# Attention over 32 memory slots and a SwiGLU layer: where the normalised x of the second pair of batches is formed

## The chip, the cores and the metric

The kernel runs on one core of a Trainium2 chip. The metric is the device time of one execution in microseconds. The engines are named as in the profile: PE multiplies matrices (PEld loads its weights), DVE is the vector engine, ACT the scalar engine, POOL is GpSimd, and SP issues nearly all DMAs. [...]

## The reference

```python
a   = softmax(phi)                       # 8 batches, 8 heads, 576 tokens, 32 slots
k_m = einsum('bhsm,bhsd->bhmd', a, k)    # memory keys and values, 64 wide
v_m = einsum('bhsm,bhsd->bhmd', a, v)
attn = softmax(q @ k_m.T / 8)            # 576 x 32 for each head
x    = (attn @ v_m), heads side by side  # 4608 tokens x 512
xn   = x / sqrt(mean(x * x) + 1e-6) * rms_g
out  = (silu(xn @ w_gate) * (xn @ w_val)) @ w_out     # 1536 hidden units
```

The kernel never forms x in full. The mean of x squared is a quadratic form of the attention weights `a` with the gram matrix of v_m; the products of v_m with the weights of the layer are formed first and the attention weights, scaled with the inverse root, are applied to those. "Pair 1's x" below means this: transposing the attention weights of a pair (`tp`, `at`), multiplying them by the gram (`xp`), squaring and summing (`ssq`), the inverse root (`rinv`), spreading it over the tokens (`rp`), scaling `at`, and splitting it into a high and a low part (`ath`, `atl`).

## The kernel before

The eight batches form four pairs, 0 to 3. The kernel has two parts.

The first stage goes through the batches. For each one it takes the softmax of phi, forms the kv product (`kvp`, L573 and L588, with `sums` of the exponentials `es`), scales and transposes it (`post1`, L596 to L605; `turn`, L617; `post2`, L627 to L633), and forms the gram (`post3`, L651 to L659). Pairs 2 and 3 leave their memory values and gram in DRAM (`vgd`, `gd`). For pairs 0 and 1 the stage also takes the scores and the softmax over slots (`q_steps`, `score_steps`; the last step, L746, writes the attention weights), and then forms their x with `x_steps`. The attention weights of both pairs stand in two SBUF tiles, a0 and a1. Meanwhile the first two slices of the weights, which come as 64-bit numbers, are read and converted (`convert`, L345 to L403) to a high and a low part.

The sweep has 48 steps. Step i works on one slice of 128 hidden units and one pair: the first 24 steps on pairs 0 and 1, two steps on pair 0, then two on pair 1, and so on; the other 24 on pairs 2 and 3. A step multiplies v_m by the weights (`vp`, L840), splits the result (`xh` on ACT, L853; `xl` on DVE, L854), forms gate and value (`pg`, `pv`, L876), the activation and product (L884, L885) and their split (`hh`, `hl`, L898 and L899). After each two steps the output products (`po`, L918) are added up (`acc`, L925). In the first half of the sweep the other weights are converted too, and attention for pairs 2 and 3 is done in small pieces (`attend_steps`); their attention weights go to DRAM (`a_dram`, L1013). The x of these two pairs comes from DRAM in three fetches (`x2`, L1029) in the course of the sweep, with PSUM from tag `o`, which the output products use as well.

The order is written down as times: each small step is put into a list with a number (`K_AT`, `X_AT`, `XB` and so on, in arbitrary units), the list is sorted, and the framework orders each engine's instructions from it, letting one that is ready pass one that is not. Tiles of one tag share buffers. SBUF and PSUM of the first stage are handed to the sweep tile by tile, when the last user is done; within a pool, memory is laid out in the order in which tags first appear. In `x2` the fetched attention weights take the buffers of `qr`, `qT` and `ex`. The 33 first events of `x_steps` (gram, fetches, transposes, products, squares, inverse root) are put at `XB + XS * number`, the last nine (spreading, scaling, splitting) at `XM + XN`.

Of the kernel before, what the change touches and what calls it, by code (L numbers as in the profile page):

```python
# [8 lines left out]
F32 = mybir.dt.float32  # L9
# [4 lines left out]
ALU = mybir.AluOpType  # L14
# [4 lines left out]
XTTR = True  # L19
WB = 3  # L20
PRM = dict(
    K_AT=[12.08, 15.05, 41.68, 67.52, 100.72, 122.69, 147.6, 167.28],
    KP=0.82,
    POST=[-0.15, 3.05, 3.9, 7.72, 15.27, 21.96],
    P1=4.13,
# [10 lines left out]
    OL=3.83,  # L36
    QO=[-0.32, 1.73, -1.7, 0.7, 1.27, 3.23],
    SO=[3.76, 13.53, 20.6, 28.62],
    X_AT=[102.5, 152.9],
    XP=1.78,  # L40
    LAG=0.79,
    CV=114.79,
# [2 lines left out]
    CP2=0.05,  # L45
    QE=[0, 0],
    CE=[2, 1],
    XE=[28, 29, 14, 13],
    ESN=[3, 3, 2, 3, 3, 3, 2, 3],
    SUM=[1, 0, 1, 0, 2, 1, 2, 1],  # L50
    CA=1,
# [10 lines left out]
    PSW=[1.728, 2.047, 2.009, 2.653, 2.96, 3.24],  # L62
    SU=[1.874, 3.014, 5.716, 6.6, 9.746, 12.208, 13.357, 15.533],
    AO=[0.162, 0.169, 0.192, 0.276, 0.385, 0.474, 0.562, 0.581, 0.59, 0.601, 0.728, 0.804, 1.158, 1.217],
    XB=[17.199, 22.916],
    XS=[0.1086, 0.0359],
    XM=[21.887, 24.858],
    XN=[0.012, 0.176, 0.184, 0.33, 0.33, 0.566, 0.596, 0.699, 0.766],
    LV=[22.571, 24.198],
    CB=1,  # L70
# [20 lines left out]
def kernel(  # L91
# [36 lines left out]
    G = 2  # L128
# [8 lines left out]
    gram = {}  # L137
    gb = persist.tile([P, 2, 2, P], F32, name="gb")
    dram = ctx.enter_context(tc.tile_pool(name="dram", bufs=1, space=bass.MemoryType.DRAM))
    gram_dram = {i: dram.tile([P, 2, 2, 64], F32, name=f"gd{i}") for i in range(G, NP)}  # L140
    a_dram = {i: dram.tile([P, NT, 256], F32, name=f"ad{i}") for i in range(G, NP)}
    rinv = [persist.tile([P, NT], F32, name=f"rinv{i}") for i in range(NP)]
    at_hi, at_lo = {}, {}

# [9 lines left out]
    def split_v(b, vg):  # L154
        pr, j = divmod(b, 2)
        for e in range(2):
            o = e ^ j
            src = vg.rearrange("p (c e) m -> p c e m", e=2)[:, :, o, :]
            hi, lo = vm[pr][:, 0, :, e, o, :], vm[pr][:, 1, :, e, o, :]
            nc.scalar.copy(hi, src)  # L160
            nc.gpsimd.tensor_tensor(out=lo, in0=src, in1=hi.bitcast(F32), op=ALU.subtract)

    def x_steps(pr, a, psum_t, psum_x, fetch=None):
# [4 lines left out]
        def first():  # L168
            st["at"] = persist.tile([P, NT, 2, P], F32, tag="at", name=f"at{pr}")
            ssqs[pr] = persist.tile([P, NT], F32, tag=f"ssq{i}", name=f"ssq{pr}")  # L170
            for par in range(2):
                rows = slice(64 * par, 64 * par + 64)
                (nc.scalar.copy if pr < G else nc.sync.dma_start)(gb[rows, :, :, rows], gram[pr][rows])

        def turn(t0):
            n = min(2, NT - t0)
# [251 lines left out]
    with ExitStack() as c1:  # L428
# [10 lines left out]
            for c in range(2):  # L439
                nc.vector.memset(hmask[32 * g:32 * g + 32, c:c + 1], float(g % 2 == c))  # L440

        a_tiles = [sb.tile([P, NT, 256], F32, name=f"a{i}", bufs=1) for i in range(G)]

        e_bd = [sk.tile([P, HP, NT, 64], F32, name=f"e_bd{i}", bufs=1) for i in range(2)]
        nc.vector.memset(e_bd[0], 0.0)
# [116 lines left out]
        def kv_steps(b):  # L562
# [84 lines left out]
            def post3():  # L647
                pr = b // 2
                if pr not in gram:
                    gram[pr] = sb.tile([P, 2, 2, 64], F32, tag="gram", name=f"gram{pr}", bufs=3)  # L650
                nc.scalar.copy(gram[pr][:, j], st.pop(("vt", b))[1][:, 0, :2])  # L651
                if pr < G:
                    if pr not in vm:
                        new_vm(pr)
                    split_v(b, st.pop(("vg", b)))
                else:
                    nc.sync.dma_start(vg_dram[b], st.pop(("vg", b)))
                    if j:
                        nc.sync.dma_start(gram_dram[pr], gram[pr])  # L659
                        gram[pr] = gram_dram[pr]  # L660
# [37 lines left out]
        def score_steps(pr, s):  # L698
            R = 2 * NT

            def mm():
                qT = st.pop(("qT", pr, s))
                sp = ps.tile([P, 1024], F32, tag="S", name=f"S{pr}_{s}", bufs=PRM["B"][2])
                for t in range(NT):
                    for j in range(2):
                        nc.tensor.matmul(
                            sp[64 * j:64 * j + 64, 64 * t:64 * t + 64],
                            qT[:, t, j::2],
                            st["km", 2 * pr + j][:, s, :],
                            start=True, stop=True,  # L710
                        )
# [12 lines left out]
            def exp():  # L724
                ex = st["ex", pr, s]
                nc.scalar.activation(ex, ex, AF.Exp, scale=SCALE)

            def norm():
                ex = st.pop(("ex", pr, s))
                sm = sb.tile([P, R, 1], F32, tag="sm", name=f"sm{pr}_{s}")  # L730
                how = PRM["SUM"][pr * HP + s]
                if how == 0:
                    nc.vector.tensor_reduce(out=sm, in_=ex, axis=AX.X, op=ALU.add)
                else:
                    half = sb.tile([P, R, M // 2], F32, tag="half", name=f"half{pr}_{s}", bufs=1)
# [10 lines left out]
                nc.gpsimd.tensor_tensor(  # L746
                    out=a_tiles[pr][:, :, 64 * s:64 * s + 64].rearrange("p t (h m) -> p t h m", m=M),
                    in0=ex.rearrange("p (t h) m -> p t h m", h=2),
                    in1=sm.rearrange("p (t h) o -> p t h o", h=2).broadcast_to([P, NT, 2, M]),
                    op=ALU.mult,  # L750
                )
# [39 lines left out]
        for pr in range(G):  # L791
            for s in range(HP):
                t = PRM["S_AT"][pr * HP + s]
                steps = q_steps(pr, s)
                ev.append((t - PRM["QL"] - PRM["OL"] - PRM["QD"][pr * HP + s], lambda pr=pr, s=s: load_q(pr, s)))
                ev.append((t - PRM["QL"] - PRM["OL"], steps[0]))
                ev += place(t - PRM["QL"], PRM["QO"], steps[1:])
                ev += place(t, PRM["SO"], score_steps(pr, s))
            if pr < G:
                ev += [(PRM["X_AT"][pr] + PRM["XP"] * p, f) for p, f in x_steps(  # L800
                    pr, lambda t, pr=pr: a_tiles[pr][:, t], tile_of("tr"), tile_of("kx"))]
        close = K_AT[B - 1] + 6 * PRM["KP"] + 0.1
        ev.append((close, lambda: (c1k.close(), late_weights())))
        w = first_weights()
# [216 lines left out]
    def x2(pr):  # L1021
        got = {}

        def fetch(t):
            def f():
                for tag, t0, n in (("qr", 0, 4), ("qT", 4, 4), ("ex", 8, 1)):
                    if t0 == t:
                        a = sb.tile([P, n, 256], F32, tag=tag, name=f"ain{pr}_{t0}")
                        nc.sync.dma_start(a, a_dram[pr][:, t0:t0 + n])  # L1029
                        for k in range(n):  # L1030
                            got[t0 + k] = a[:, k]
            return f
        steps = x_steps(pr, got.pop, o_tile, o_tile, fetch)
        return [f for _, f in steps]
# [30 lines left out]
            ev.append((p + 2.01 * PRM["PI"], ld))  # L1065
    for a, p in enumerate(PRM["SU"]):
        ev += place(p, PRM["AO"], attend_steps(G + a // HP, a % HP))
    for a in range(NP - G):
        steps = x2(G + a)
        n = len(steps) - 9  # L1070
        ev += [(PRM["XB"][a] + PRM["XS"][a] * x, f) for x, f in enumerate(steps[:n])]
        ev += place(PRM["XM"][a], PRM["XN"], steps[n:])
        ev.append((PRM["LV"][a], lambda a=a: late_vm(G + a)))
    for _, f in sorted(ev, key=lambda e: e[0]):
        f()
# [30 lines left out]
```

## Time and profile before

| | us |
|---|---|
| median of 3 runs (908.34 to 909.11) | 908.46 |
| the profiled execution | 907.8 |
| its span in the trace | 906.0 |
| PE busy | 837.0 |
| DVE busy | 575.7 |
| first kv, attention and x work (first stage) | to about 146 |
| first gate product of the sweep | 154.3 |

A row of a time line gives start, duration, engine, line and operation, tiles as out<-in, and in brackets the engine's idle time before it and what ended that. A row of a group gives line, engine, operation, tiles and shapes, the count, busy us and mean ns of one, then the idle time before. A row of stages gives the window, its length, the busy us (and number of instructions) of PE, PEld, DVE, ACT and POOL, the granted clock of PE, the mean DMA share and GB/s.

### The profile page before, as it was taken

The page shows a single profiled execution, that of the slowest core. Times are in us where ns is not written, and L with a number is a line of the kernel's source. Part 1 is how long each engine was busy: PE and PEld are TensorE (multiplying, and loading weights), DVE is VectorE, ACT ScalarE, POOL GpSimd, SP SyncE. Part 2 cuts the span into 40 slices and gives each one's busy share as a digit, 9 for nine tenths or more (in the row PEclk, how much of TensorE's full clock was granted, in tenths as well). Part 3 has the DMA queues.
Part 4 walks back from the last instruction along what each step waited for, and adds up shares of the span by engine and source line. Part 5 has one row for each costly group of instructions (what it writes and reads, how often), then busy time and mean ns, then how long its engine had stood idle before and what let it go on. Part 6 is the DMA issues. An engine that isn't in the chain of part 4 may idle for free.

```text
span 906.0 us, 15847 instructions
## 1 busy us (share of the span) xinstructions
PE 837.0 (92%) x6207; PEld 744.5 (82%) x6207; DVE 575.7 (64%) x994; ACT 420.2 (46%) x717; POOL 326.2 (36%) x274
## 2 busy tenths in 40 slices
PE   4998485899998899999999999999999999999997
PEld 4776474788986798888898997799899999999996
DVE  5577959896788777877855656532445455454543
ACT  2666334787765355664642443254424333233330
POOL 3464735553636245344532331411212121121120
PEclk9899787999999999999999999999999999999999
DMA  8986554454445332543413133501204013040046
GB/s 277 337 278 209 201 166 120 168 146 107 164 133 162 101 119 84 152 114 103 140 57 129 52 88 118 121 31 47 94 1 140 1 47 93 1 140 1 1 114 142
DMA packets 81506, 106.41 MB, mean 117 GB/s; under 512 B 34324, under 2 KB 52248, under 8 KB 81432
## 3 DMA queue, kind: packets, MB, share of 16 engines
q1 hardware_dynamic: 81432, 105.41, 37.6%
q8 instruction: 49, 0.80, 0.4%
q14 instruction: 25, 0.20, 0.1%
HBM read 73.93 MB, written 31.46 MB: 116 GB/s over the span
## 4 chain that ended last, share of the span: by engine, by line
PE 73%; DVE 14%; DMA 4%; ACT 3%; issue 3%; POOL 2%; SPq 1%; POOLq 0%; ACTq 0%; DVEq 0%
PE po L918 30%; PE pv L876 15%; PE pg L876 15%; PE vp L840 7%; DMA phi<-in_phi_dram 2%; PE xp L235 2%; DVE mi L365 1%; DVE mi L369 1%; DVE xl L854 1%; DVE ex L345 1%; PE kvp L573 1%; DMA q<-in_q_dram 1%; DVE ex L347 1%; DVE acc L925 1%; SPq L298 1%
## 5 line engine op out<-in xcount | busy, mean ns | idle before, releaser
L899 POOL TENSOR_TENSOR hl<-hf,hh 128x512 fp32r<-128x512 f32 (+1 forms) x96 | 139.8, 1457 | 361.3 <-ACT hh L898 353.3
L925 DVE TENSOR_TENSOR acc<-po,acc 128x512 f32<-128x512 f32 x180 | 123.0, 687 | 128.0 <-PE po L918 127.2
L918 PE MATMUL po<-oh,hh 128*128 128x512 f32 x432 | 173.5, 403 | 8.3 <-DVE acc L925 5.2
L918 PE MATMUL po<-oh,hl 128*128 128x512 f32 x432 | 171.3, 397 | 0.0
L918 PE MATMUL po<-ol,hh 128*128 128x512 f32 x432 | 171.0, 396 | 0.0
L884 ACT ACTIVATE sg<-pg 128x256 f32<-128x256 f32 x192 | 78.2, 409 | 171.2 <-PE pg L876 150.0
L854 DVE TENSOR_TENSOR xl<-vp,xh 64x1024 fp32r<-64x1024 f32 x96 | 117.1, 1220 | 48.1 <-ACT xh L853 47.0
L885 DVE TENSOR_TENSOR hf<-pv,sg 128x256 f32<-128x256 f32 x192 | 85.5, 453 | 79.1 <-PE pv L876 51.6
L853 ACT CAST xh<-vp 64x1024 fp32r<-64x1024 f32 x96 | 96.6, 1007 | 53.6 <-PE vp L840 25.5
L918 PEld LDWEIGHTS po<-oh,hh 128*128 128x128 f32 x432 | 81.5, 189 | 23.5 <-DVE acc L925 7.5
L898 ACT CAST hh<-hf 128x512 fp32r<-128x512 f32 (+1 forms) x96 | 64.6, 673 | 77.0 <-DVE hf L885 54.2
L918 PEld LDWEIGHTS po<-oh,hl 128*128 128x128 f32 x432 | 81.4, 189 | 19.4
L876 PE MATMUL pg<-ath,xh 128*128 128x320 f32 (+1 forms) x384 | 86.6, 300 | 8.5 <-ACT xh L853 6.0
L918 PEld LDWEIGHTS po<-ol,hh 128*128 128x128 f32 x432 | 81.7, 189 | 11.1
L840 PE MATMUL vp<-wh,vm 128*128 128x256 f32 x384 | 86.9, 289 | 3.5 <-DVE at L212 2.3
L876 PE MATMUL pv<-ath,xh 128*128 128x320 f32 (+1 forms) x384 | 84.8, 300 | 3.2 <-DVE hf L885 3.1
L876 PE MATMUL pg<-atl,xh 128*128 128x320 f32 (+1 forms) x384 | 85.0, 297 | 0.0
L876 PE MATMUL pg<-ath,xl 128*128 128x320 f32 (+1 forms) x384 | 84.8, 295 | 0.0
L876 PE MATMUL pv<-atl,xh 128*128 128x320 f32 (+1 forms) x384 | 84.5, 297 | 0.0
L876 PE MATMUL pv<-ath,xl 128*128 128x320 f32 (+1 forms) x384 | 84.1, 297 | 0.0
L876 PEld LDWEIGHTS pg<-ath,xh 128*128 128x128 f32 x384 | 63.6, 191 | 14.1 <-ACT xh L853 6.6
L840 PEld LDWEIGHTS vp<-wh,vm 128*128 128x128 f32 x384 | 66.8, 193 | 6.2 <-DVE at L212 2.5
(129 smaller groups left out, 1394.6 us busy)
## 6 DMA issues: line engine op xcount, KB each, us to landing
kv<-in_k_dram SPq DMA_DIRECT2D x32, 288.0 KB, 5.0
kv<-in_v_dram SPq DMA_DIRECT2D x32, 288.0 KB, 5.6
out_dram<-acc SPq DMA_DIRECT2D x72, 128.0 KB, 2.4
raw<-in_moe_w_gate_dram SPq DMA_DIRECT2D x12, 512.0 KB, 3.9
raw<-in_moe_w_val_dram SPq DMA_DIRECT2D x12, 512.0 KB, 3.7
wd<-wh SPq DMA_DIRECT2D x12, 512.0 KB, 3.0
wd<-wl SPq DMA_DIRECT2D x12, 512.0 KB, 4.5
raw<-in_moe_w_out_dram SPq DMA_DIRECT2D x12, 512.0 KB, 3.5
```

The costliest lines, as they stand in the source:

```text
L235: nc.tensor.matmul(xp[64 * j:64 * j + 64, P * cc:P * cc + P], st["at"][:, t, cc, 64 * j:64 * j + 64], gb[:, j, cc], start=True, stop=True,)
L298: issued.append(nc.sync.dma_start(out, in_).ins)
L840: nc.tensor.matmul(vp[:, cc, e, :], lhs(l), r[:, 2 * cc + e, :], start=(n == 0), stop=(n == 2),)
L853: nc.scalar.copy(xh[rows], src)
L854: nc.vector.tensor_tensor(out=xl[rows], in0=src, in1=xh[rows].bitcast(F32), op=ALU.subtract)
L876: nc.tensor.matmul(pt[:, :N], l[:, cc, b, half * P:half * P + P], r[:, b, cc, t0:t0 + n, :].rearrange("p t x -> p (t x)"), start=(m == 0), ...
L884: nc.scalar.activation(sg[:, :N], pg[:, :N], AF.Silu)
L885: nc.vector.tensor_tensor(out=hf[:, :, b, :], in0=pv[:, :N].rearrange("p (t x) -> p t x", x=64), in1=sg[:, :N].rearrange("p (t x) -> p t x ...
L898: nc.scalar.copy(hh, hv)
L899: nc.gpsimd.tensor_tensor(out=hl, in0=hv, in1=hh.bitcast(F32), op=ALU.subtract)
L918: nc.tensor.matmul(po, l[:, tt, :], r, start=(m == 0), stop=(m == 5))
L925: nc.vector.tensor_tensor(out=accs[key], in0=po, in1=accs[key], op=ALU.add)
```

## The change

Pair 1's attention weights no longer stay in SBUF. POOL scales them in place and SP writes them to `a_dram[1]`, 64 columns for each s; its gram is written to `gram_dram[1]` behind batch 3. The tile a1 is gone. Pair 1's `x_steps` are taken out of the first stage (`X_AT` has one entry) and called through `x2`, as those of pairs 2 and 3 are: the first 33 events are put at -1.1 to 0.5 of the sweep, in its units of steps, behind the first half of step 0's L840, and the last nine at 0.61 to 1.37. Steps 0 and 1 use pair 0; step 2 is the first one on pair 1. The gram's block matrix `gb` is filled by two DMAs instead of two ACT copies. One of the copies of transposed weights moves from DVE to ACT (`XE`), and batches 6 and 7 are put at 146.0 and 166.6 instead of 147.6 and 167.28.

```diff
-    K_AT=[12.08, 15.05, 41.68, 67.52, 100.72, 122.69, 147.6, 167.28],
+    K_AT=[12.08, 15.05, 41.68, 67.52, 100.72, 122.69, 146.0, 166.6],
-    X_AT=[102.5, 152.9],
+    X_AT=[102.5],
-    XE=[28, 29, 14, 13],
+    XE=[28, 31, 14, 13],
-    XB=[17.199, 22.916],
-    XS=[0.1086, 0.0359],
-    XM=[21.887, 24.858],
+    XB=[-1.1, 17.199, 22.916],
+    XS=[0.05, 0.1086, 0.0359],
+    XM=[0.6, 21.887, 24.858],
...
-    gram_dram = {i: dram.tile([P, 2, 2, 64], F32, name=f"gd{i}") for i in range(G, NP)}
-    a_dram = {i: dram.tile([P, NT, 256], F32, name=f"ad{i}") for i in range(G, NP)}
+    gram_dram = {i: dram.tile([P, 2, 2, 64], F32, name=f"gd{i}") for i in range(1, NP)}
+    a_dram = {i: dram.tile([P, NT, 256], F32, name=f"ad{i}") for i in range(1, NP)}
...
-                (nc.scalar.copy if pr < G else nc.sync.dma_start)(gb[rows, :, :, rows], gram[pr][rows])
+                (nc.scalar.copy if pr < 1 else nc.sync.dma_start)(gb[rows, :, :, rows], gram[pr][rows])
...
-        a_tiles = [sb.tile([P, NT, 256], F32, name=f"a{i}", bufs=1) for i in range(G)]
+        a0 = sb.tile([P, NT, 256], F32, name="a0", bufs=1)
...
                     split_v(b, st.pop(("vg", b)))
+                    if pr and j:
+                        nc.sync.dma_start(gram_dram[pr], gram[pr])
+                        gram[pr] = gram_dram[pr]
...
+                if pr == 0:
+                    nc.gpsimd.tensor_tensor(
+                        out=a0[:, :, 64 * s:64 * s + 64].rearrange("p t (h m) -> p t h m", m=M),
...
+                else:
+                    nc.gpsimd.tensor_tensor(out=ex, in0=ex, in1=sm.broadcast_to([P, R, M]), op=ALU.mult)
+                    nc.sync.dma_start(
+                        a_dram[pr][:, :, 64 * s:64 * s + 64], ex.rearrange("p (t h) m -> p t (h m)", h=2)
+                    )
...
-            if pr < G:
-                ev += [(PRM["X_AT"][pr] + PRM["XP"] * p, f) for p, f in x_steps(
-                    pr, lambda t, pr=pr: a_tiles[pr][:, t], tile_of("tr"), tile_of("kx"))]
+        ev += [(PRM["X_AT"][0] + PRM["XP"] * p, f) for p, f in x_steps(
+            0, lambda t: a0[:, t], tile_of("tr"), tile_of("kx"))]
...
-    for a in range(NP - G):
-        steps = x2(G + a)
+    for a in range(NP - 1):
+        steps = x2(1 + a)
```

More of the change, by code (lines that the diff above doesn't have):

```diff
@@ L745, in norm @@
                 nc.vector.reciprocal(sm, sm)
[L746 to L751, printed above, removed]
+                if pr == 0:
+                    nc.gpsimd.tensor_tensor(
+                        out=a0[:, :, 64 * s:64 * s + 64].rearrange("p t (h m) -> p t h m", m=M),
+                        in0=ex.rearrange("p (t h) m -> p t h m", h=2),
+                        in1=sm.rearrange("p (t h) o -> p t h o", h=2).broadcast_to([P, NT, 2, M]),
+                        op=ALU.mult,
+                    )
[3 more added lines that the diff above has]
+                        a_dram[pr][:, :, 64 * s:64 * s + 64], ex.rearrange("p (t h) m -> p t (h m)", h=2)
+                    )
             return [mm, top, exp, norm]
@@ L1072 @@
         ev += place(PRM["XM"][a], PRM["XN"], steps[n:])
+    for a in range(NP - G):
         ev.append((PRM["LV"][a], lambda a=a: late_vm(G + a)))
```

## The prediction

> **What bounds the kernel now.** I read the page first, then busy times by stage, then the order of time around the border between the first stage and the sweep.
>
> ```profile
> PE 837.0 (92%) x6207; PEld 744.5 (82%) x6207; DVE 575.7 (64%) x994; ACT 420.2 (46%) x717; POOL 326.2 (36%) x274
> ```
>
> PE is busy for 837 of 906 us. A change that leaves the arithmetic alone can only win from the other 69 us, or from PE work done at a lower clock. The stages (columns: window, its length, busy us of PE, PEld, DVE, ACT, POOL, granted clock, DMA share, GB/s) show where they lie:
>
> ```profile
> 160.00:210.00 50.00, 44.31 (x327) 40.49 (x326) 45.13 (x66) 36.06 (x65) 26.89 (x21) 1.00 0.48 146
> 119.80:210.00 90.20, 71.11 (x587) 64.08 (x586) 74.09 (x133) 52.09 (x94) 45.80 (x36) 0.91 0.50 154
> 210.00:255.00 45.00, 45.00 (x316) 41.27 (x315) 31.12 (x46) 34.31 (x62) 25.90 (x19) 1.00 0.47 148
> 255.00:300.00 45.00, 37.05 (x272) 31.57 (x272) 40.70 (x69) 26.65 (x42) 19.41 (x15) 0.99 0.48 135
> ```
>
> From 119.8 to 210 us PE idles 19.1 us and DVE 16.1. At 210 PE is the bound and DVE has 14 us to spare in 45. Between 255 and 300 PE loses 8 us more, among weight conversions. After that the sweep is PE's. So the change is decided between 120 and 210 us, and a microsecond gained on PE there should reach the end. Six rows of PE's order of time (start, duration, what, idle before it and who ended it) mark that stretch:
>
> ```profile
> 119.87 1.09 PE L184 MATMUL tp<-ident,a 128*128 128x128 f32 x8
> 133.28 1.85 PE L573 MATMUL kvp<-kv,e_bd 128*64 128x128 f32 x29
> 138.39 0.26 PE L588 MATMUL kvp<-ones,e_bd 128*64 128x1 f32 x2
> 145.67 0.54 PE L840 MATMUL vp<-wh,vm 128*128 128x256 f32 x1 [2.34 <-DVE at L212]
> 154.30 0.80 PE L876 MATMUL pg<-ath,xh 128*128 128x256 f32 x2 [5.73 <-ACT xh L853]
> 178.54 0.40 PE L876 MATMUL pg<-ath,xh 128*128 128x256 f32 x2
> ```
>
> Pair 1's x begins at 119.87 and stands ahead of batch 7's kv product (133.28 to 138.65). The sweep's first product (L840) waits for pair 1's last rescaling on DVE (L212), because its PSUM banks are those of the first stage's transposes. The first gate product follows at 154.30; the first of pair 1 (step 2) is the row at 178.54. DVE and ACT in between:
>
> ```profile
> 140.07 0.15 DVE L596 TENSOR_SCALAR si<-kvp 128x2 f32<-128x2 f32 x1
> 141.01 0.41 DVE L605 TENSOR_TENSOR vb<-kvp,im 128x256 f32<-128x256 f32 x1
> 141.34 2.34 DVE L212 TENSOR_TENSOR at<-at,rp 128x1024 f32<-128x1024 f32 x2
> 145.21 0.41 DVE L212 TENSOR_TENSOR at<-at,rp 128x256 f32<-128x256 f32 x1
> 150.11 0.99 ACT L853 CAST xh<-vp 64x1024 fp32r<-64x1024 f32 x1
> 152.00 1.21 DVE L854 TENSOR_TENSOR xl<-vp,xh 64x1024 fp32r<-64x1024 f32 x1
> ```
>
> **The change, part by part.**
>
> *The weights' and gram's way through DRAM.* Four puts, one gram store, three fetches and two gram loads join SP's queue; two ACT copies of the gram (L173) go. The sweep does the same for pairs 2 and 3 already:
>
> ```profile
> L1013 SPq DMA_DIRECT2D ad<-ex x8: 564/571/592, 205.5 to 435.4; - x8
> DMA to landing us min/median/max: 3.0/3.0/3.4
> 111.68 2.47 POOL L746 TENSOR_TENSOR a<-ex,sm 128x576 f32<-128x576 f32 x2
> ```
>
> A put costs SP 0.57 us and lands 3.0 us later. The last two weights are written by POOL at 111.7 to 114.2, so the last put lands by 118, well before the fetch (about 132, below). Behind the puts on SP stand batch 7's kv loads, of which the last goes out at 121.5 (below), seven us after the weights are there. I take 0. Without that cover two puts cost 1.1 us; a put that SP reaches before its weights are written would hold the loads by as long as it waits, 2.5 us at most if it stands there when POOL begins. The other end is a gain of nothing: no queue gets shorter. The three fetches and the gram's loads wait on SP for memory and for pair 0's products; behind them stand the sweep's first loads of q and of weights, which wait for work of the same moment. I take 0 there too; the cover gone, five issues of 0.57 us cost 2.9.
>
> *What leaves the first stage.* Pair 1's x on DVE and on PE between 119.8 and 146 (line, engine, operation, count, busy us, mean ns), and one row of the sweep for the full clock:
>
> ```profile
> L248 DVE CUSTOM_DVE_ANT_0 xp<-xp,a 128x256 f32<-128x256 f32 x9 | 3.9, 431 | 4.5 <-PE xp L235 4.4
> L248 DVE DVE_READ_ACCUMULATOR2_ANT ssq<- 128x1 f32 x9 | 1.3, 142 | 0.0
> L276 DVE SCALAR_TENSOR_TENSOR rinv<-u,rinv 128x9 f32<-128x9 f32 x4 | 1.7, 435 | 0.1
> L274 DVE TENSOR_TENSOR u<-rinv 128x9 f32<-128x9 f32 x4 | 0.7, 170 | 0.1
> ...
> L194 DVE COPY at<-tp 128x512 f32<-128x512 f32 x1 | 0.7, 680 | 0.0
> L235 PE MATMUL xp<-gb,at 128*64 128x128 f32 x72 | 7.3, 350 | 2.9 <-DVE ssq L248 2.4 <-ACT at L194 0.4
> L184 PE MATMUL tp<-ident,a 128*128 128x128 f32 x18 | 3.7, 348 | 0.0
> L204 PE MATMUL rp<-ident,rinv 128*128 128x128 f32 x9 | 1.4, 284 | 2.4 <-DVE rinv L276 2.0 <-DVE at L212 0.5
> L235 PE MATMUL xp<-gb,at 128*64 128x128 f32 x72 | 5.7, 284 | 0.2 <-DVE acc L925 0.2
> ```
>
> DVE: squares 3.9 + 1.3, copy 0.7, the inverse root 1.7 for L276 and 2.2 for thirteen others of 128x9 (at the 0.17 of L274), rescaling 2.34 + 0.41 (L212 above): 12.6 us. PE: 7.3 + 3.7 + 1.4 = 12.4 us. The last row is the same product for pair 2 in the sweep: 5.7 us at full clock instead of 7.3. With the two groups of transposes scaled alike PE's part there is 9.7 us.
>
> *When batch 7 can then run.* Its last kv load, the load's time to landing, the sums that it needs, and the next work that DVE has:
>
> ```profile
> 121.52 0.42 SPq L298 DMA_DIRECT2D kv<-in_v_dram  x1
> kv<-in_v_dram SPq DMA_DIRECT2D x3, 288.0 KB, 4.6
> 122.14 2.61 POOL L556 TENSOR_TENSOR es<-es,e_bd 128x512 f32<-128x512 f32 x2
> 128.11 0.43 DVE L345 TENSOR_SCALAR ex<-raw 128x512 int32<-128x512 int32 x1 [3.41 <-DMA raw<-in_moe_w_val_dram]
> ```
>
> 121.52 + 0.42 + 4.6 = 126.5; the sums es are there at 124.8. The kv product and its sums took 5.4 us, but its first half needs only earlier loads: done at about 130.5 instead of 138.65. DVE is free then, so si to vb (1.35 us, rows above) end near 132 and the transposes near 133, some nine us earlier than now.
>
> *When the sweep can start.* Without the rescaling in the transposes' banks, L840 can run before batch 7 is done. With a1 gone and the fetched tiles named ahead of xh, my count of tile sizes puts xh on memory of vb, so its first copy waits for batch 7's transposes: 133. From the first xh to the gate product it is 154.30 − 150.11 = 4.2 us now, so the gate product starts at about 137.2, 17 us earlier. This is not yet the gain: the 12.6 us of DVE and 9.7 of PE come back inside the first two steps.
>
> *Two books to 210 us.* DVE: the stretch holds 74.1 us of work before and 73.4 after (the edit of XE moves one copy of 0.7 to ACT). Until 130.5 DVE has only batch 6's closing work (si to vb, 1.35 as above) and a weight conversion (five instructions of 0.4 to 0.7 us, 2.6, from 128.1): it idles 6.8 us. The other 69.5 us at the share of 160 to 210, 45.13 of 50 or 0.90, end at 207.7: 2.3 us gained. At 0.95 they end at 203.7: 6.3. PE: until 137.2 it has some 9 us of its 71.1. Of the other 62.1, 2.7 go with the higher clock (12.4 against 9.7); 59.4 at 0.89 (44.31 of 50) end at 203.9, 6.1 us gained, at 0.95 at 199.7, 10. Both books allow about 6. What DVE still owes at 210 are conversions, and it has the 14 us of slack of the next window for them. I take 6.0, with 2.3 and 10 as the ends.
>
> *The clock.* At the start of the gate products the clock was low:
>
> ```profile
> 154.30:160.00 5.70, 5.70 (x29) 5.70 (x30) 4.16 (x6) 3.29 (x5) 2.52 (x2) 0.55 1.02 316
> ```
>
> At 0.55 these 5.7 us cost some 2.5 against full speed, behind an idle of 5.7 us. After the change PE still waits for xh, so I count no gain; if pair 1's transposes fill that wait, 2.5 more. [...]
>
> *The rest.* K_AT moves batches 6 and 7 less than 2 units ahead in the order; they wait for loads: 0. The stall of 255 to 300 hangs on conversions against steps, both shifted alike: 0, with ±3 as its ends.
>
> **The sum.** 907.8 us is the profiled execution's time (span 906.0), 0.7 under the median of 908.46. 907.8 − 6.0 = 901.8, so 902.5 against the median.
>
> **The rivals.**
>
> *Nothing gained.* Pair 1's POOL work collides with conversions in the sweep as it does now:
>
> ```profile
> 143.48 5.78 POOL L224 TENSOR_TENSOR atl<-at,ath 128x512 fp32r<-128x512 f32 x4
> 150.63 1.76 POOL L224 TENSOR_TENSOR atl<-at,ath 128x128 fp32r<-128x128 f32 x2
> 146.63 1.50 DVE L365 TENSOR_SCALAR mi<-raw 128x512 int32<-128x512 int32 x1
> 161.28 0.42 DVE L365 TENSOR_SCALAR mi<-raw 128x512 int32<-128x512 int32 x1
> ```
>
> The same DVE instruction takes 0.42 us alone and 1.50 beside the subtraction. In the first steps POOL also has the conversions' and hidden layer's subtractions, so DVE's share of useful time falls: 69.5 us at 0.88, two hundredths under the present share, end at 209.5, a gain of 0.5; with the 0.7 to the median 908.0. For it speaks that DVE is as full as PE from 160 to 210; against it, that PE can do output products while a gate product waits, and that fewer of these collisions are left ahead of the first gate product, where the 1.50 stood. [...]
>
> *Slower: pair 1's x comes too late for step 2.* Its chain now runs from 119.87 to the end of the last subtraction, 150.63 + 1.76 = 152.4: 32.5 us. In the sweep it shares the two PSUM banks of the output products. Pair 3's there:
>
> ```profile
> L184 PE MATMUL tp<-ident,ain x18: 272/273/332, 539.1 to 560.3; 128*128 128x128 f32 x18
> L224 POOL TENSOR_TENSOR atl<-at,ath x12: 458/1296/1313, 519.8 to 583.2; 128x512 fp32r<-128x512 f32 x8, 128x128 fp32r<-128x128 f32 x4
> ```
>
> From 539.1 to 583.2 and the last subtraction's 0.5: 44.6 us. A fetch issued at 132 lands at about 135, if it takes the 3.0 us of the put. From there 43.5 us reach 178.54, step 2's present start: a longer chain makes the change a loss. At 48 us it costs 4.5: 913. Against it: pair 3's was spread over several steps by XS, pair 1's is written densely.
>
> *A larger gain.* PE without a gap from 137.2: 59.4 us end at 196.6, 13.4 gained: 895.1 against the median.
>
> **Chances.** About 6 us faster (899 to 905, with the books' ends 898.5 to 906): 0.56. Larger gain 0.12. Nothing gained 0.16. Slower 0.16. Differences under 0.2% (1.8 us) cannot be told from none here; the nothing case and the forecast's low end split about it: faster 0.70, same 0.13, slower 0.17. The range takes half of the larger gain and part of the slow rival: 895.5 to 911.
>
> **What would show it.** Right: the first gate product at 135 to 142; batch 7's kv product ending near 130; L840 not waiting for L212; the first gate product of pair 1 before 173; 210 to 300 unchanged but for the shift. Wrong: L345 or L365 at 1.2 us and more through the first three steps and PE waiting for xl or hf; the first pair 1 product waiting for L224; kv loads later than 122 behind a put; a longer stall than 8 us after 250.

## The result and the profile after

The changed kernel takes 929.03 us (median of four runs, 926.8 to 933.15) against 908.6 for the kernel before beside it: ratio 1.0234, 95% interval 1.0203 to 1.0265. That is 20 us slower, where 6 us faster was forecast and 911 was the upper end. The profiled execution is the longest of the four (933.15 us, span 931.4).

The same views as before the change, of the changed kernel. Its lines are L848 for `vp`, L861 and L862 for `xh` and `xl`, L884 for `pg` and `pv`, L893 for `hf`, L926 for `po`, L1037 for the fetches; the x steps and the conversions keep their numbers. First the page's busy times, then busy times by stage:

```profile
PE 851.7 (91%) x6207; PEld 755.9 (81%) x6207; DVE 581.2 (62%) x993; ACT 422.8 (45%) x716; POOL 326.0 (35%) x274
```

```profile
160.00:210.00 50.00, 33.56 (x196) 29.11 (x194) 42.18 (x72) 25.40 (x47) 24.16 (x19) 0.73 0.45 135
255.00:300.00 45.00, 41.65 (x278) 38.03 (x279) 33.08 (x49) 29.73 (x51) 20.73 (x16) 0.92 0.41 126
```

From 160 to 210 us PE is busy for 33.6 us instead of 44.3, and its clock is at 0.73 instead of 1.00. DVE is nearly as busy as before (42.2 against 45.1). The window from 255 to 300 loses less than before (3.4 us of PE idle against 8.0) only because the stall that stood there now comes at about 319. PE's order of time:

```profile
125.99 6.29 PE L573 MATMUL kvp<-kv,e_bd 128*64 128x128 f32 x72
136.10 0.38 PE L848 MATMUL vp<-wh,vm 128*128 128x256 f32 x1
142.30 0.79 PE L884 MATMUL pg<-ath,xh 128*128 128x256 f32 x2 [4.51 <-ACT xh L861]
145.88 1.07 PE L184 MATMUL tp<-ident,ain 128*128 128x128 f32 x4
166.50 0.90 PE L884 MATMUL pv<-ath,xh 128*128 128x320 f32 x2 [3.21 <-DVE hf L893]
176.88 1.09 PE L235 MATMUL xp<-gb,at 128*64 128x128 f32 x16 [2.18 <-ACT at L194]
190.78 1.94 PE L204 MATMUL rp<-ident,rinv 128*128 128x128 f32 x8 [6.55 <-DVE rinv L276]
194.43 0.79 PE L884 MATMUL pg<-ath,xh 128*128 128x256 f32 x2 [0.17 <-ACT ath L223]
197.01 0.78 PE L926 MATMUL po<-oh,hh 128*128 128x512 f32 x1
```

Batch 7 and the first gate product (142.30, was 154.30) come early, as meant. Pair 1's x then runs from 145.88 to past 194, and its first gate product (194.43) is 16 us later than before the change. The first output product (197.01) stands behind all of x's tiles, although its operands were there by 175. DVE in the last part of that chain:

```profile
172.93 0.42 DVE L248 CUSTOM_DVE_ANT_0 xp<-xp,ain 128x256 f32<-128x256 f32 x1
173.28 0.14 DVE L248 DVE_READ_ACCUMULATOR2_ANT ssq<- 128x1 f32 x1
173.28 1.88 DVE L369 SCALAR_TENSOR_TENSOR mi<-raw,mi 128x512 f32<-128x512 uint32 x1
175.34 1.22 DVE L862 TENSOR_TENSOR xl<-vp,xh 64x1024 fp32r<-64x1024 f32 x1 [0.19 <-ACT xh L861]
176.49 1.24 DVE L358 SCALAR_TENSOR_TENSOR ex<-raw,ex 128x512 int32<-128x512 int32 x1
177.65 0.42 DVE L248 CUSTOM_DVE_ANT_0 xp<-xp,ain 128x256 f32<-128x256 f32 x1
...
179.92 1.50 DVE L345 TENSOR_SCALAR ex<-raw 128x512 int32<-128x512 int32 x1
...
184.08 1.12 DVE L265 TENSOR_SCALAR rinv<-m 128x9 int32<-128x9 int32 x1
...
190.46 0.17 DVE L276 SCALAR_TENSOR_TENSOR rinv<-u,rinv 128x9 f32<-128x9 f32 x1
```

Between one pair of squares (L248) and the next stand pieces of a weight conversion. Not all of the delay arises on DVE itself. The ACT copy of the third pair of transposes starts at 165.73, behind a conversion's L350 that waited 2.33 us for L347 on DVE, and PE forms the products from it (L235) at 171.54, behind gate products that had waited 3.21 us for `hf` (the row at 166.50). Both of these waits end at a DVE instruction that stands in or behind a conversion. The groups of one conversion instruction on DVE, each from 119.8 to step 2's first gate product, first of the changed kernel (to 194.43), then of the kernel before (to 178.54):

```profile
L369 DVE SCALAR_TENSOR_TENSOR mi<-raw,mi 128x512 f32<-128x512 uint32 x10 | 11.3, 1126 | 0.0
```

```profile
L369 DVE SCALAR_TENSOR_TENSOR mi<-raw,mi 128x512 f32<-128x512 uint32 x6 | 5.2, 859 | 0.0
```

Ten conversions now run on DVE ahead of step 2, not six. Six of the ten stand between x's first square (151.95) and its first rescaling (192.51). How the steps move, by the fourth activation of the gate in a step (us, one profiled execution each; the runs are explained below):

| step | before | after | e4 | e5 | e6 | e8 | e10 | e17 |
|---|---|---|---|---|---|---|---|---|
| 1 | 177.6 | 170.2 | 164.6 | 170.6 | 163.9 | 163.1 | 160.9 | 163.6 |
| 2 | 188.9 | 207.6 | 195.3 | 210.4 | 199.9 | 191.0 | 171.0 | 173.5 |
| 4 | 220.7 | 233.6 | 225.5 | 237.1 | 229.2 | 218.4 | 228.4 | 198.8 |
| 6 | 249.4 | 271.7 | 264.0 | 261.9 | 261.8 | 254.6 | 260.3 | 256.8 |
| 9 | 304.7 | 326.7 | 318.1 | 316.7 | 313.3 | 305.6 | 313.9 | 312.4 |

After the change step 1 is 7 us ahead and step 2 is 19 us behind. From step 9 on the difference stays at 22 us up to step 29, and it is 25 us at the end. Two cautions go with the table. One execution can stand some 4 us off: on DVE e12 (below) has the order of the kernel before up to 286 us and still passes step 1 at 181.4. And a mark says nothing of the other work done by then: since 119.8 the changed kernel has run 293 matmuls at step 1's mark, the kernel before 362, so the 7 us are no lead. At step 2's mark both have run nearly as many (first the kernel before, then the changed one):

```profile
119.80:188.86 69.06, 52.40 (x447) 47.41 (x447) 54.69 (x104) 37.95 (x70) 36.09 (x29) 0.88 0.50 156
```

```profile
119.80:207.59 87.79, 60.28 (x441) 53.74 (x442) 75.09 (x126) 45.84 (x80) 44.32 (x36) 0.75 0.52 163
```

So 18.7 of the 22 us are lost by step 2. Of these, 10.8 are time in which PE idles (27.5 us, was 16.7), and 7.9 are nearly the same work at a lower clock (0.75, was 0.88). The low stretches lie around and behind waits of PE: 0.52 in the 5.1 us behind the wait of 3.21, and 0.50 from 180 to 195, around the wait of 6.55. Step 6 is 9 us further behind than step 4, but PE idles for only 3.3 us between these two marks; 243 matmuls run there instead of 182, work that had been put off.

### The profile page after: what moved, and what is told of

Same layout as the page of the kernel before. It is cut to its first block, busy times and chain, and to the rows that moved or that the text cites. A ratio compares the mean times of both kernels' runs of the same rounds, so it can differ in the third digit from the quotient of the medians.

```text
span 931.4 us, 15867 instructions
## 1 busy us (share of the span) xinstructions
PE 851.7 (91%) x6207; PEld 755.9 (81%) x6207; DVE 581.2 (62%) x993; ACT 422.8 (45%) x716; POOL 326.0 (35%) x274
## 4 chain that ended last, share of the span: by engine, by line
PE 71%; DVE 15%; DMA 4%; issue 4%; ACT 3%; POOL 2%; SPq 0%; POOLq 0%; DVEq 0%; ACTq 0%
PE po L926 29%; PE pv L884 15%; PE pg L884 14%; PE vp L848 6%; PE kvp L573 3%; DVE mi L369 2%; DMA phi<-in_phi_dram 2%; DVE ex L345 2%; DVE mi L365 1%; DVE xl L862 1%; DVE ex L347 1%; DMA oh<-od 1%; PE xp L235 1%; POOL w L385 1%; DVE acc L933 1%
## 5 line engine op out<-in xcount | busy, mean ns | idle before, releaser
L933 DVE TENSOR_TENSOR acc<-po,acc 128x512 f32<-128x512 f32 x180 | 123.0, 687 | 131.2 <-PE po L926 130.5
L926 PE MATMUL po<-oh,hh 128*128 128x512 f32 x432 | 175.7, 408 | 7.3 <-DVE acc L933 4.8
L926 PE MATMUL po<-oh,hl 128*128 128x512 f32 x432 | 172.4, 399 | 0.0
L926 PE MATMUL po<-ol,hh 128*128 128x512 f32 x432 | 172.1, 398 | 0.0
L862 DVE TENSOR_TENSOR xl<-vp,xh 64x1024 fp32r<-64x1024 f32 x96 | 117.1, 1220 | 54.3 <-ACT xh L861 53.2
L893 DVE TENSOR_TENSOR hf<-pv,sg 128x256 f32<-128x256 f32 x192 | 85.7, 453 | 94.0 <-PE pv L884 61.0
L861 ACT CAST xh<-vp 64x1024 fp32r<-64x1024 f32 x96 | 96.7, 1008 | 53.9 <-PE vp L848 30.4
L926 PEld LDWEIGHTS po<-oh,hh 128*128 128x128 f32 x432 | 82.6, 192 | 23.4 <-DVE acc L933 7.0
L926 PEld LDWEIGHTS po<-oh,hl 128*128 128x128 f32 x432 | 82.2, 190 | 20.0
L884 PE MATMUL pv<-ath,xh 128*128 128x320 f32 (+1 forms) x384 | 87.1, 306 | 7.8 <-DVE hf L893 7.7
L884 PE MATMUL pg<-ath,xh 128*128 128x320 f32 (+1 forms) x384 | 88.7, 305 | 5.5 <-ACT xh L861 4.5
L926 PEld LDWEIGHTS po<-ol,hh 128*128 128x128 f32 x432 | 82.7, 191 | 11.3
L848 PE MATMUL vp<-wh,vm 128*128 128x256 f32 x384 | 86.8, 288 | 1.1 <-DVE xl L862 0.8
L884 PE MATMUL pg<-atl,xh 128*128 128x320 f32 (+1 forms) x384 | 85.9, 300 | 0.0
L884 PE MATMUL pv<-atl,xh 128*128 128x320 f32 (+1 forms) x384 | 85.7, 301 | 0.0
L884 PE MATMUL pg<-ath,xl 128*128 128x320 f32 (+1 forms) x384 | 85.6, 297 | 0.0
L884 PE MATMUL pv<-ath,xl 128*128 128x320 f32 (+1 forms) x384 | 85.0, 299 | 0.0
L884 PEld LDWEIGHTS pv<-ath,xh 128*128 128x128 f32 x384 | 65.3, 195 | 13.3 <-DVE hf L893 8.7
L884 PEld LDWEIGHTS pg<-ath,xh 128*128 128x128 f32 x384 | 65.2, 194 | 11.4 <-ACT xh L861 4.9
```

Of the source, the lines that this page charges most:

```text
L848: nc.tensor.matmul(vp[:, cc, e, :], lhs(l), r[:, 2 * cc + e, :], start=(n == 0), stop=(n == 2),)
L861: nc.scalar.copy(xh[rows], src)
L862: nc.vector.tensor_tensor(out=xl[rows], in0=src, in1=xh[rows].bitcast(F32), op=ALU.subtract)
L884: nc.tensor.matmul(pt[:, :N], l[:, cc, b, half * P:half * P + P], r[:, b, cc, t0:t0 + n, :].rearrange("p t x -> p (t x)"), start=(m == 0), ...
L893: nc.vector.tensor_tensor(out=hf[:, :, b, :], in0=pv[:, :N].rearrange("p (t x) -> p t x", x=64), in1=sg[:, :N].rearrange("p (t x) -> p t x ...
L926: nc.tensor.matmul(po, l[:, tt, :], r, start=(m == 0), stop=(m == 5))
```

## The experiments

Theory A: step 2 waits for pair 1's x, and x is late because its instructions on DVE stand among conversions. Later it takes in the output products, held by x's tiles in the two shared PSUM buffers (A+). PSUM is the memory of the kernel's pools `ps1` and `ps2`, which PE writes (`vp`, the row at 136.10) and ACT and DVE read (`xh` at 138.97, `xl` at 175.34). Rival B: the trip through DRAM. Rival C: the sum of the work in the first steps, whatever its order. Each ratio is to the kernel before on the same chip, whose medians were 907.8 to 908.8.

| run | median us | ratio, 95% interval |
|---|---|---|
| e1_trip | 923.17 | 1.0168 (1.0129 to 1.0207) |
| e2_sbuf | 923.20 | 1.0160 (1.0134 to 1.0185) |
| e3_nowait | 922.40 | 1.0158 (1.0142 to 1.0173) |
| e4_behind | 919.65 | 1.0132 (1.0102 to 1.0162) |
| e5_po | 918.12 | 1.0116 (1.0094 to 1.0137) |
| e6_both | 912.11 | 1.0051 (1.0035 to 1.0066) |
| e7_nowait_po | 918.66 | 1.0122 (1.0098 to 1.0147) |
| e8_sbuf_both | 906.64 | 0.9971 (0.9956 to 0.9987) |
| e9_numbers | 922.79 | 1.0141 (1.0101 to 1.0180) |
| e10_nowait_both | 917.55 | 1.0087 (1.0058 to 1.0115) |
| e11_order17 | 903.30 | 0.9941 (0.9911 to 0.9971) |
| e12_before17 | 903.34 | 0.9939 (0.9918 to 0.9961) |
| e13_nowait_att | 916.49 | 1.0090 (1.0064 to 1.0117) |
| e14_both_att | 911.70 | 1.0038 (1.0018 to 1.0058) |
| e15_best_att | 909.24 | 1.0005 (0.9990 to 1.0021) |
| e16_before_att | 906.24 | 0.9987 (0.9965 to 1.0010) |
| e17_nowait_s3 | 915.44 | 1.0090 (1.0070 to 1.0111) |
| e18_best_s2 | 904.35 | 0.9955 (0.9930 to 0.9980) |

### The trip alone, and the change without it

e1 adds the trip to the kernel before and leaves the x of pair 1 in the first stage:

```diff
+    nc.sync.dma_start(a_dram[pr][:, :, 64 * s:64 * s + 64], ...)   # as in the change
+    # x_steps of pair 1, ahead of the first transposes:
+    nc.sync.dma_start(a_tiles[1][:, t:t + 4], a_dram[1][:, t:t + 4])
```

> The kernel before with one part of the change alone: pair 1's weights go to DRAM as they are written, its gram too, and both are fetched again into a1 for the x of the first stage, which stays where it was. Theory A (step 2 waits for pair 1's x, whose instructions stand in DVE's order between weight conversions, so that its chain takes 57 us instead of 32.5): the trip costs nothing much, 906 to 912. Rival B (the trip is the loss: the weights come back late, and everything behind them on SP): 915 or more, x's first transposes several us behind 119.87. Rival C (crowding: DVE and PE work put into the dense stretch costs there, whoever waits for whom): 906 to 912, as A.

e2 is the changed kernel without the trip of the weights (its gram still goes through DRAM):

```diff
-    nc.gpsimd.tensor_tensor(out=ex, in0=ex, ...); nc.sync.dma_start(a_dram[pr]..., ex...)
+    a1 = persist.tile([P, NT, 256], F32, tag="ath1", name="a1")   # written as a0 is
-    steps = x_steps(pr, got.pop, o_tile, o_tile, fetch)
+    x_steps(1, lambda t: a1[:, t], o_tile, o_tile, ...)
```

> The changed kernel with pair 1's weights kept in SBUF (in the memory that ath of pair 1 takes later), no trip, no fetch; x still in the sweep. Theory A: the first transposes can start when PSUM is free, at 137 to 142 instead of 145.88, so step 2's first gate product comes at most 4 to 9 us before 194.4, and the time is 917 to 930: most of the 20 us stays. Rival B: back to 905 to 911. Rival C: 920 to 930.

e1 missed its expectation: the trip alone, placed so, costs 15 us (923.17). SP's queue and PE's order in e1:

```profile
130.66 0.33 SPq L298 DMA_DIRECT2D raw<-in_moe_w_out_dram  x1
131.08 0.86 SPq L811 DMA_DIRECT2D a<-ad  x2
...
135.79 1.94 PE L184 MATMUL tp<-ident,a 128*128 128x128 f32 x8 [12.88 <-DMA a<-ad]
```

The fetch stands on SP behind a load of weights that waits for its buffer until 130.66. PE idles 12.88 us, and x starts at 135.79 instead of 119.87. In the changed kernel the trip costs less, 5.8 us (929.0 to 923.2 in e2): the rest of the loss is there without it. e2's chain starts 6 us earlier and ends hardly earlier:

```profile
140.02 0.97 PE L185 MATMUL tp<-ident,a 128*128 128x128 f32 x4
...
189.44 1.94 PE L205 MATMUL rp<-ident,rinv 128*128 128x128 f32 x8 [5.31 <-DVE rinv L277]
```

So rival B (the trip) is not the main loss. In e2, too, PE waits for the root on DVE at the chain's end (5.31 us).

### Taking the wait away

```diff
-    ah, al = at_hi[pr], at_lo[pr]
+    ah, al = (at_hi[0], at_lo[0]) if i in (2, 3) else (at_hi[pr], at_lo[pr])
```

> The changed kernel in which steps 2 and 3 (the first two on pair 1) multiply by pair 0's ath and atl instead of pair 1's, so that their output is another one; pair 1's x is formed as before, with all its work, but first used in step 6. Theory A: no wait at step 2, its first gate product at 170 to 176; the time falls to 897 to 911, 911 if the second loss, 9 us at step 6, stays as it is. Rival C: all the work is still there, so most of the loss stays: 918 to 930.

Theory A missed: 922.4. Step 2 came at 180.2 (was 207.6) and step 3 at 191.1. PE got to the middle of step 4 by 197.7 and was then busy for 5.2 of 13.4 us, with the first output product at 211.10, behind x's last tiles; step 4 was through at 228.0:

```profile
201.50 0.53 PE L848 MATMUL vp<-wh,vm 128*128 128x256 f32 x1 [3.84 <-DVE xl L862]
...
211.10 0.79 PE L926 MATMUL po<-oh,hh 128*128 128x512 f32 x1 [2.66 <-DVE at L212]
```

Without the wait of the gate product 6.6 of the 20 us come back; it alone does not carry the loss.

### Two rules of order

e4 puts the DVE instructions of four conversions behind x's root. The added line is an order on one engine, not a wait for another:

```diff
+    root[pr] = nc.vector.scalar_tensor_tensor(out=r, ...).ins      # L276, the last one
+    if (kind, n) in ((0, 2), (1, 2), (0, 3), (1, 3)):
+        with tc.issue_after(root[1]): s0(); ...                     # also s1, s2
```

> The changed kernel with one more rule on DVE's order: the DVE instructions of the conversions of slices 2 and 3 (gate and value) stand behind the last instruction of pair 1's inverse root. Nothing waits for another engine for it, nothing is left out. Theory A: x's chain loses the 4 conversions that ran ahead of its end (about 4 x 4.2 us of DVE as measured in 119.8 to 194.4), the last root instruction comes near 176 instead of 190.46, step 2's first gate product near 180 instead of 194.43, and the time falls by 6 to 18 us, to 910 to 923. Rival C (the sum of DVE's work is what counts, not its order): the conversions come later and are waited for in steps 4 to 6 instead; 925 to 935, step 2 earlier but the lag at step 8 the same 22 us.

e5 writes four output products of steps 0 and 1 ahead of x's last nine events, so that they come first in the two shared PSUM buffers:

```diff
-    XM=[0.6, ...                 # rp, scaling, splitting
+    XM=[1.34, ...
-    ev += place(i + 1, PRM["O"], out_steps(i))
+    ev += place(i + 1, [t / 100 - 0.72 for t in range(4)] + PRM["O"][4:] if i == 1 else PRM["O"], out_steps(i))
```

(The last step of the conversions of w_out slices 0 and 1 is written earlier for it, at 1.21 and 1.22.)

> The changed kernel with the first four output products of steps 0 and 1 (two steps' 24 matmuls, some 5.7 us of PE at full clock) written ahead of the last nine events of pair 1's x, so that they get their turn in the two shared PSUM buffers before rp and not behind it; x's place on DVE is unchanged. Theory A+ (x's chain is late, and the output products that could fill PE's wait stand behind it in the order of the shared PSUM buffers): PE works on po from about 181 instead of idling 6.55 us ahead of rp, the root ends at 190 as in the changed kernel, and 4 to 8 us come back: 920 to 926. If only the lateness of x counts and po is then missing later: no change, 926 to 932.

e6 has both:

> The changed kernel with both edits: conversions of slices 2 and 3 behind the root on DVE (as in the run e4_behind, 919.65), and four output products ahead of rp (as in e5_po). Theory A+: the wait ahead of rp (4.15 us with the first edit alone) is filled, 912 to 918. If the loss has moved into the conversions, which now come later and share DVE with steps 2 to 6: 917 to 924.

e4 gains 9.4 us, e5 10.9 (more than the 4 to 8 expected), e6 16.9. The rows of `rp` in e4, and of the end of the chain in e5 and e6:

```profile
177.04 1.94 PE L205 MATMUL rp<-ident,rinv 128*128 128x128 f32 x8 [4.15 <-DVE rinv L277]
```

```profile
191.58 0.62 PE L204 MATMUL rp<-ident,rinv 128*128 128x128 f32 x4 [0.19 <-DVE rinv L276]
```

```profile
179.29 0.60 PE L205 MATMUL rp<-ident,rinv 128*128 128x128 f32 x4
```

In e4 `rp` comes 13.7 us earlier, as expected, and PE still idles 4.15 us for it. In e5 the root is as late as before, but the wait of 6.55 is down to 0.19. In e6 both are gone. No work was taken out, so order alone brings back 17 of the 20 us.

e8 is e6 without the trip of the weights (e2's edit):

> The run e6_both without the trip: pair 1's weights stay in SBUF. The first transposes then start at about 140 instead of 145.9 to 147.4, and with the chain no longer stretched by conversions the root should end 5 to 7 us before that of e6_both. Theory A+: 3 to 7 us below e6_both, 906 to 914. If the start does not matter: equal to e6_both within 3 us.

906.64: 5.5 us under e6 and 0.3% under the kernel before. x starts at 137.66, and `rp` comes at 174.54:

```profile
137.66 0.60 PE L186 MATMUL tp<-ident,a 128*128 128x128 f32 x4
...
174.54 0.60 PE L206 MATMUL rp<-ident,rinv 128*128 128x128 f32 x4
```

### The two small numbers

```diff
-    K_AT=[..., 146.0, 166.6],   XE=[28, 31, 14, 13],
+    K_AT=[..., 147.6, 167.28],  XE=[28, 29, 14, 13],
```

> The changed kernel with the two small edits of numbers undone: batches 6 and 7 at 147.6 and 167.28 again (K_AT), and one copy of transposed weights on DVE again instead of ACT (XE). If they are side issues, as the prediction counted them: 925 to 933, the loss unchanged. If they carry part of the loss: 920 or less; if they had softened it: 935 or more.

e9 takes 922.79, between the outcomes that were written down. The numbers that were counted as 0 carry 6 us here; the order on DVE and PE changes with them, and the share of each of the two was not tried apart. They do not cost this in every order: e8 has both edits and is no slower than the kernel before.

### Where the loss goes without the wait

e7 is e3 with e5's edit, and e10 is e6 with e3's:

> The changed kernel in which steps 2 and 3 multiply by pair 0's ath and atl instead of pair 1's (another output), and in which four output products stand ahead of rp. Without the second edit steps 0 to 3 were through by 191 and PE then idled, since all output products stood behind x in the shared PSUM buffers; the time was 922.4. Theory A+: with both waits on x gone, the time falls to 902 to 914. Rival C (the sum of the work, or DVE's full book, is the bound): 918 or more.

> The run e6_both (conversions of slices 2 and 3 behind the root on DVE, four output products ahead of rp; 912.1), in which steps 2 and 3 multiply by pair 0's ath and atl (another output), so that no gate product waits for pair 1's x before step 6. If the wait of step 2 itself still costs: 902 to 908. If what costs is that x's work and the conversions share DVE and PE with the first steps, whoever waits (rival C): 909 to 915, no better than e6_both.

Both missed theory A: 918.7 and 917.6, the first no better than e5 (918.1), the second 5 us worse than e6 (912.1). In e10 steps 0 to 3 are through at 184, and then PE idles, for instance here (DVE, then PE):

```profile
194.61 1.49 DVE L346 TENSOR_SCALAR ex<-raw 128x512 int32<-128x512 int32 x1 [2.05 <-POOL w L386]
196.01 1.48 DVE L366 TENSOR_SCALAR mi<-raw 128x512 int32<-128x512 int32 x1
...
199.27 1.35 DVE L359 SCALAR_TENSOR_TENSOR ex<-raw,ex 128x512 int32<-128x512 int32 x1
200.54 0.48 DVE L1009 TENSOR_TENSOR ex<-S,mx 128x320 f32<-128x320 f32 x1
...
201.17 0.77 PE L934 MATMUL po<-oh,hh 128*128 128x512 f32 x1 [4.40 <-DVE ex L1009]
```

An output product waits for a PSUM buffer that a piece of attention holds, and its release on DVE (L1009) stands behind a conversion. e13 and e14 move the first two pieces of attention away, in e10 and in e6:

```diff
-    SU=[1.874, 3.014, ...
+    SU=[3.4, 4.4, ...
```

> The run e10_nowait_both (917.6: no gate product waits for pair 1's x before step 6, conversions behind the root, four output products ahead of rp) with the first two pieces of attention for pair 2 put later (3.4 and 4.4 instead of 1.874 and 3.014), so that their tiles no longer stand between output products in the two shared PSUM buffers. In e10_nowait_both PE idled 4.40 us at 201.17 for an output product behind such a piece, whose DVE instruction stood behind a conversion. Theory A++ (the two buffers are handed over in a written order, and each handover waits for a DVE or ACT instruction that stands behind conversions; the wait of step 2 is only one of the forms of that): 905 to 912. If the load of DVE and PE in the first steps is what counts (rival C): 914 to 920.

> The run e6_both (912.1) with the same two pieces of attention put later. Theory A++: fewer handovers among the output products of steps 0 to 5, 905 to 911. Rival C: 910 to 915; the pieces come back into later steps, so a gain can be given back there, where the attention is wanted for pair 2 by the middle of the sweep.

A miss: 916.5 and 911.7, no change that can be told. Another candidate was slice 2, which the rule of e4 makes late for step 4. e17 holds back slice 3 alone in e10 (the list of e4's rule is `((0, 3), (1, 3))`):

> The run e10_nowait_both (917.6) in which only the conversions of slice 3 are held behind the root, not those of slice 2. In e10_nowait_both slice 2 (gate and value) was converted to the end at 200.1, 25 us later than in the kernel before, and step 4, its first user, came at 209.0 (first xl) although steps 0 to 3 were through at 184. If what takes the place of the wait at step 2 is a wait of step 4 for slice 2, because DVE cannot do both x and slice 2 in time: step 4 some 10 us earlier and 905 to 912. If slice 2 is then early but x late again and nothing is won: 914 to 920, with PE idle where x's last steps are waited for.

Step 4 came at 198.8 instead of 228.4, yet step 5 at 238.5, and the time is 915.4, by the ratios the same as e10's. Its waits of PE from 180 to 240:

```profile
PE pv L892 <- DVE hf L901: 5.7, 3, 4.9
PE po L934 <- DVE ex L1009: 4.7, 1, 4.7
```

The waits move from one instruction behind a conversion to the next. So rival C is half right: what the gate products gain by running ahead is lost again. In part it is no gain: at step 3's mark (183.8) e10 has run 467 matmuls since 119.8, the kernel before 585 at its own (208.2), so part of the earlier work is still owed. Rival C is not the whole, as e4 to e6 gain 17 us with the same work. Which of DVE's debts is the last one in the runs without the wait stays open.

### A stall that the kernel before has, too

The stall near 290 to 300 us is in the kernel before, too: PE waits 3.42 us for `acc`, which stands behind a conversion of slice 7 (DVE, then PE):

```profile
296.86 0.68 DVE L369 SCALAR_TENSOR_TENSOR mi<-raw,mi 128x512 f32<-128x512 uint32 x1
297.46 0.68 DVE L925 TENSOR_TENSOR acc<-po,acc 128x512 f32<-128x512 f32 x1
...
298.19 0.49 PE L918 MATMUL po<-oh,hh 128*128 128x512 f32 x1 [3.42 <-DVE acc L925]
```

e11 (on e8) and e12 (on the kernel before) put that conversion behind step 8's last `hf`:

```diff
+    if (kind, n) == (1, 7):
+        with tc.issue_after(h8[8, 1, 1]): s0(); ...    # hf of step 8, second group, second half
```

> The run e8_sbuf_both (906.6) with one more rule on DVE's order: the conversion of slice 7's value weights, which stood ahead of step 8's last hf and of an acc (PE idle 3.40 us at 298.20, <-DVE acc), stands behind that hf. Theory A+ (DVE's order, not its load, makes these stalls): 2 to 6 us less, 901 to 905. If DVE's load is what counts: the stall moves on, 905 to 908.

> The kernel before with the same one rule on DVE's order alone (slice 7's value weights behind step 8's last hf), to keep its gain apart from that of the other edits; the kernel before has the same stall at 298.19 (3.42 us). Theory A+: 903 to 907; if the stall moves on: 907 to 910.

903.30 and 903.34. From 285 to 300 in the kernel before and in e12 (whose profiled execution runs 3.9 us later up to there):

```profile
285.00:300.00 15.00, 10.28 (x45) 7.35 (x44) 14.86 (x23) 7.95 (x12) 8.64 (x7) 0.98 0.47 153
```

```profile
285.00:300.00 15.00, 12.33 (x71) 9.92 (x72) 11.26 (x22) 7.69 (x11) 5.53 (x5) 1.00 0.55 142
```

From step 8's mark to step 10's e12 takes 40.5 us, the kernel before 46.8. One rule is worth some 5 us in the kernel before, and 3.3 in e8. With it the two arrangements are equal: x in the sweep, at its best here, gains nothing over x in the first stage. The edit of attention on top of each (e15, e16), and e11 with slice 2's gate weights not held back (e18: the list is `((1, 2), (0, 3), (1, 3))`):

> The run e11_order17 (903.3) with the same two pieces of attention put later. Theory A++: 898 to 903. Rival C: 902 to 906.

> The run e12_before17 (903.3: the kernel before with slice 7's conversion behind step 8's hf) with the same two pieces of attention put later. In the kernel before the first stage's x uses other PSUM buffers, and PE idles little between 160 and 290, so there is less to win: 901 to 905 by theory A++, the same by rival C; above 905 if the pieces collide with conversions where they now stand.

> The run e11_order17 (903.3: no trip, conversions behind the root, four output products ahead of rp, slice 7's conversion behind step 8's hf) in which slice 2's gate weights are not held behind the root, only its value weights and slice 3. Slice 2 should be ready some 8 us before 195.6. If step 4's wait for slice 2 still costs in the best version: 899 to 902; if x's chain, which then has one conversion more in it, gives it back: 903 to 907.

None is an improvement: 909.2 (5.9 us slower than e11), 906.2 and 904.4. The fastest are e11 and e12.

## Why the prediction was wrong

- **The way through DRAM, taken as 0.** It costs 5.5 us (e6 to e8) to 5.8 (after to e2). The puts did not delay batch 7's kv loads. The last put left SP at 121.53, seven us later than the prediction has it but still well before the fetch. The fetch went out at 139.45 instead of 132 and took 6.5 us to land instead of the put's 3.0, beside weights that kept the DMA share at 0.99:

```profile
138.00:145.00 7.00, 2.70 (x12) 2.70 (x13) 5.92 (x8) 4.41 (x6) 2.74 (x2) 0.69 0.99 311
```

```profile
139.45 1.83 SPq L1037 DMA_DIRECT2D ain<-ad  x3
```

```profile
ain<-ad SPq DMA_DIRECT2D x2, 512.0 KB, 6.5
```

- **Batch 7 at 130.5, and L840 not waiting for L212:** right in kind. The product and its sums ended at 133.1 (POOL had the sums `es` at 130.05 instead of 124.8), and L848 ran at 136.10 with no wait for L212.
- **The first gate product at 137.2:** it came at 142.30, 12.0 us earlier than before and not 17, behind a wait of 4.51 us for `xh`. The first `xh` ran at 138.97 instead of 133: its product, L848, stood on PE behind batch 7's gram (to 136.1), and ACT waited 1.12 us ahead of it for a conversion's L369 on DVE. The clock was low there (0.69 from 138 to 145, row above; 0.54 in the 5.7 us from 142.30, as 0.55 before), and no gain was counted for it. The 2.5 us that the prediction names for a filled wait stay its estimate. Behind a shorter wait, too, the clock was low: 0.52 in the 5.1 us behind the 3.21 us ahead of 166.50.
- **The two books to 210 us: the step that failed.** DVE's book was nearly right as a sum (0.84 busy from 160 to 210, where 0.90 to 0.95 was assumed). A sum does not say which instruction comes when, and here DVE did not let a ready instruction pass a waiting one: it idles 0.86 us for PE ahead of the `hf` at 171.72, while L347 of a conversion, whose operand was there at 170.00, runs behind it at 172.60. DVE ran four more conversions ahead of step 2, and x's chain took 57 us from its first transpose to its last subtraction (145.88 to 203.0) instead of the 32.5 of the first stage:

```profile
195.74 7.29 POOL L224 TENSOR_TENSOR atl<-at,ath 128x512 fp32r<-128x512 f32 x6
```

  PE's book assumed that PE stays at 0.89 to 0.95 of the time at full clock. The cover that it needs is named in the rival "nothing gained", output products while a gate product waits, and was not checked there. They could not fill the wait: they took the two shared PSUM buffers in the written order, behind x (e5). PE was at 0.67, with its clock at 0.73.
- **The numbers `K_AT` and `XE`, taken as 0:** 6.2 us (e9).
- **The stall of 255 to 300, ±3:** it came again 22 us later. Ahead of it PE idles 3.2 us more in step 6, where `hf` stood behind a conversion (DVE, then PE):

```profile
270.43 0.68 DVE L369 SCALAR_TENSOR_TENSOR mi<-raw,mi 128x512 f32<-128x512 uint32 x1
271.03 0.48 DVE L893 TENSOR_TENSOR hf<-pv,sg 128x320 f32<-128x320 f32 x1
...
271.57 0.80 PE L884 MATMUL pv<-ath,xh 128*128 128x256 f32 x2 [3.23 <-DVE hf L893]
```

- **The rival "too late for step 2"** had the place right (194.43 is past 178.54), with a chance of 0.16. It put the start at 135 (145.88) and the price at the lateness of x alone. The 44.6 us that it read from pair 3 fit the chain once the conversions of slices 2 and 3 stand behind its root: 42.8 in e4, 44.6 in e6. e3, e7 and e10 show that this wait is not all that the loss consists of.

## What to carry to other kernels

When work is moved next to other work, a book of busy times gives a bound and not a forecast: follow each engine's order, and ask of every wait which instruction stands ahead of the one that ends it. Cover must be checked at its buffers: work that could fill a gap does not, if its tiles come after the late ones in a shared buffer. A changed order is cheap to try, and with no work changed it was worth 5 to 17 us here, while the move itself, in the best order found for it, gained nothing.

## What was not expected of the hardware

An instruction of DVE on 128x9, 0.17 us alone, took 1.12 beside one of POOL (DVE's is L265 above, from 184.08 to 185.20):

```profile
183.90 1.27 POOL L385 TENSOR_TENSOR w<-mi,ex 128x512 f32<-128x512 f32 x1 [2.77 <-DVE m L259]
```

POOL's ends at 185.17, DVE's 0.03 us behind it. The last but one L276 of the same root (1.12 us from 188.90) ends 0.03 us behind the next L385 (188.73 and 1.26 us) in the same way. So in these two cases a small step of a dependent chain paid for a collision about as much as a large one did (0.95 us more each, 1.08 more for the L365 of 128x512 that the prediction shows).
